# Beta loaded behind the second x segment, and the order of work planned anew

## The chip, the cores and the metric

The kernel runs on one core of a Trainium2 chip. The metric is the device time of one execution in microseconds (us), median over several runs. The engines of the core run their own instruction queues and meet through semaphores: PE does matrix products, DVE and ACT elementwise work (ACT also exponentials and the GELU), POOL elementwise work on SBUF, and SP does nothing but issue DMAs here. PE writes to PSUM, which DVE and ACT read; POOL and the DMAs do not touch it in this kernel.

## The reference

Two branches over the same x (2048 tokens, 512 features) are mixed per token by a gate. Branch A is attention in four segments of 512 tokens with 32 heads of 16, plus a linear memory (M, z) of the earlier segments; `beta` (32 numbers) mixes memory and attention per head. Branch B is a gated feed-forward layer with 1792 hidden features.

```python
g = sigmoid((x * gate_w).sum(-1, keepdims=True))
# branch A, per segment s of 4
qs, ks, vs = q[:, :, s], k[:, :, s], v[:, :, s]
p = softmax(qs @ ks^T * 0.25 + causal_mask)
a_dot = p @ vs
pq = phi(qs)                                  # phi(t) = t + 1 if t > 0 else exp(t)
a_mem = (pq @ M) / (pq @ z + 1e-06)
o = sigmoid(beta) * a_mem + (1 - sigmoid(beta)) * a_dot
M = M + phi(ks)^T @ vs ; z = z + phi(ks).sum(tokens)
a = o @ wo
# branch B
b = (gelu(x @ w_gate) * (x @ w_up)) @ w_down
out = g * a + (1 - g) * b
```

All inputs and the output are bf16.

## The kernel before

The whole sequence stays on the chip: weights, one to three segments of x transposed (`xT`, three buffers), and all intermediate tiles. Work is cut into named tasks of one to 128 instructions. The names are segment and index:

- `K`, `Q`: one of four feature blocks of a projection, 4 matmuls of 128x512 each; `V0_1b`: one of eight value groups (4 matmuls of 256 or 257 columns; the 257th is the token gate, from gate_w). K of segment 0 is cut into parts a, b, c that follow the arrival of x. `Kev`, `Qev`, `Vev` are the evictions from PSUM, on DVE (`:d`) or ACT (`:a`).
- `kpada`, `kpadb` (DVE): K with half of its partitions masked, needed by the scores. `phka`, `phkb`, `phkc`: the three steps of phi(K) (DVE L460, ACT L462, DVE L464); `ktr` its DMA transpose, L572. `phq...` the same for Q.
- `st0_1B` (PE, L601): one fill of score columns into the four banks of `psX`; `exp0_1B` (ACT, L608) its exponential into a `pt` tile, `msk0_1B` (POOL, L614) the causal mask on it. There is one `psX`: the next fill waits for the exponential. A segment has 18 fills. `pv0_1` (PE, L643): the probability-value product of two feature blocks, 128 small matmuls; it needs the masks and `vsh`, a copy of V shifted by 64 partitions, made by DMA (L517). Then `tp`, `pvp`, `ota` (DVE: L529, L666 and L667, L672), where L667 multiplies by `gq` = 1 - sigmoid(beta).
- `mz`, `mza`, `mzq`: memory write; `nd` (PE, L546), `ndp` (DVE, L557 to L560), `otr` (DMA, L563), `otm` (DVE, L674): memory read. L557 uses `gfull`, that is from beta too.
- `G`, `U`: one of 14 hidden blocks of w_gate (`wg`) and w_up (`wu`), 4 matmuls each; `Gev`, `gelu`, `gd`, `h`: eviction, GELU, product. `out0_1_0`: a third of a row block of the product with w_down. `wev`: its eviction times 1 - g; `wo`: product with wo; `oev` (L752) joins both; `dma` stores. Row block 15, the last, is cut into two halves (`wo3_3a`, `wo3_3b`).

All PE products except the scores go through four PSUM banks (`psD`); the digit behind a task in the order is the bank that it opens. A bank can be opened again when its last reader is through.

Nothing is ordered at run time: the string `ORDER`, at the end of the file, lists all tasks, and every engine issues its own tasks in that order. The Emitter adds the semaphore waits that the data require. So a task waits for what it needs and all tasks behind it on the same engine wait with it. The string is the result of an offline planner.

The loads: `ld_x0_1` and `ld_wk0` are issued by ACT, all others by SP. A load can be told to wait for another to have landed (the list at the end of `ld_w`), if that other one stands earlier in the order. Of x, the first two row blocks of segment 0 are transposed on PE (`xtr0`, evicted by `xev0`), all else by DMA transposes (`ld_x0_t2`, `ld_x0_t3`, `ld_x1_0` to `ld_x3_3`). Halves of the weights are `wk0`, `wk1`, `wq0` and so on. `ld_x2_...` waits for `wu1`, `ld_wg0` and `ld_wu0` for `wq1`, `ld_wv` for `x0_t3`, `ld_wu1` for `wg0`.

The gating instructions of beta: `betab` (DVE, L763, four copies), `bexp` (ACT, two exponentials, L775 and L776), `gqa` (POOL), `gqb` (DVE), `gfull` (POOL). Those of the token gate: `gwz`, `ld_gw`, `gwtr`, `gwev` put gate_w into column 512 of wv; `gz`, `gr`, `goa`, `gob`, `goc` make g and 1 - g per segment.

The order of the loads on SP's queue before is: x0_0, wk1, x0_t2, x0_t3, wq0, wq1, gw, beta, wv, wg0, x1_2, x1_1, x1_3, x1_0, wu1, x2_0, vsh0_21, x2_1, x2_3, ktr0_3, wg1, vsh0_01, vsh0_20, x2_2, ktr0_2, vsh0_00, wd1, wd0, wu0, ktr0_1, ktr0_0, and later ones.

Of the kernel before, what the change touches and what calls it, by code (L numbers as in the profile page):

```python
# [876 lines left out]
G1_2:1 U0_0:0 gd0_7 Gev1_2:d pvp0_11 h0_0 U0_13:3 U0_10:2 h0_10 Q2_1:1 Qev2_1:d exp0_2C st0_2D mz0:0 U0_7:2 U0_9:1
pvp0_10 h0_13 exp0_2D phqb1_0 st0_2E exp0_2E phka1_0 h0_7 mza0 h0_9 ota0_0 phqa1_2 kpadb1_0 G1_4:3 U0_1:2 h0_1
Gev1_4:a V1_1b:0 st0_3A G1_0:1 U0_5:3 Q2_2:2 exp0_3A Vev1_1b:a Gev1_0:a Qev2_2:a kpadb1_1 st0_3B exp0_3B U0_11:0
U0_4:1 U0_12:2 st0_3C phkb1_0 exp0_3C phqc1_0 kpada1_2 h0_4 h0_5 U0_6:1 U0_2:3 h0_11 h0_12 phqb1_2 h0_2 G1_3:0  # L880
Gev1_3:d h0_6 kpadb1_2 st0_3D phka1_2 U0_3:2 h0_3 U0_8:3 h0_8 Q2_3:0 Qev2_3:d exp0_3D phkb1_2 msk0_2A msk0_2B msk0_2C
msk0_3A msk0_2E msk0_2D msk0_3C goc0 msk0_3B st1_0A msk0_3D pv0_3:1230 exp1_0A st1_0B exp1_0B tp0_d20 tp0_d21 pvp0_20
tp0_d30 ota0_1 pvp0_21 tp0_d31 kpada1_3 out0_1_0:1 out0_1_1 out0_1_2 V2_0a:2 Vev2_0a:d G1_9:3 V2_1b:0 Vev2_1b:d
wev0_1:d st1_0C G1_8:2 G1_10:0 G1_11:1 gelu1 gd1_9 G1_7:3 gd1_8 gd1_10 gd1_7 gd1_11 G1_13:2 gd1_13 G1_12:0 gd1_12
phqc1_2 phkc1_0 mzq0 pvp0_31 pvp0_30 ota0_3 V2_0b:3 Vev2_0b:d ota0_2 V2_1a:1 Vev2_1a:d out0_0_0:2 out0_0_1 out0_0_2
nd1_0:0 ndp1_0 phkc1_2 exp1_0C st1_0D exp1_0D K2_0:3 K2_2:1 wev0_0:d Kev2_0:d Kev2_2:a K2_1:0 st1_0E Kev2_1:d U1_2:2
h1_2 wo0_1:1 nd1_3:3 nd1_1:0 exp1_0E st1_1A ld_x3_2 vsh1_00 vsh2_01 ktr1_1 ktr1_0 oev0_1 ndp1_1 wo0_0:2 oev0_0
kpada2_0 vsh1_21 out0_2_0:1 nd1_2:0 msk1_0C msk1_0A exp1_1A st1_1B exp1_1B msk1_0B gz1 msk1_0E msk1_1A msk1_0D msk1_1B
out0_2_1 wo0_2:2 ndp1_2 st1_1C exp1_1C nd1_5:0 out0_2_2 ndp1_3 wev0_2:a ndp1_5 out0_3_0:3 st1_1D nd1_4:0 out0_3_1
out0_3_2 ktr1_2 dma0 vsh1_01 otr1_3 ndp1_4 otr1_0 oev0_2 phka2_0 msk1_1C wev0_3:d ktr1_3 dma1 vsh2_00 otr1_1 ld_x3_1  # L890
ld_x3_0 ld_x3_3 exp1_1D st1_2A exp1_2A gr1 msk1_1D pv1_1:1023 st1_2B exp1_2B tp1_d01 tp1_d00 kpadb1_3 V2_2b:0
Vev2_2b:d K2_3:1 Kev2_3:a G2_3:0 pvp1_00 Gev2_3:d tp1_d10 st1_2C U1_8:1 G2_1:0 otr1_2 V2_3a:2 h1_8 Gev2_1:d Vev2_3a:d
kpadb2_0 kpadb2_1 exp1_2C st1_2D phkb2_0 exp1_2D G2_6:1 wo0_3:0 U1_3:2 pvp1_01 tp1_d11 Gev2_6:a h1_3 phka2_2 oev0_3
st1_2E U1_0:3 V2_3b:1 G2_0:2 Gev2_0:d h1_0 Vev2_3b:d exp1_2E phkb2_2 st1_3A mz1:0 G2_4:2 G2_5:3 pvp1_10 mza1 Gev2_5:d
exp1_3A st1_3B exp1_3B Gev2_4:d U1_11:1 G2_2:0 Gev2_2:d ota1_0 U1_13:3 h1_13 U1_10:2 h1_10 h1_11 G2_11:0 G2_10:3
pvp1_11 phkc2_0 phkc2_2 ota1_1 otm1_0 otm1_1 G2_12:2 G2_9:1 st1_3C gelu2 gd2_11 gd2_12 G2_7:0 G2_13:2 gd2_10 gd2_9
gd2_7 gd2_13 G2_8:3 gd2_8 U1_7:1 U2_9:0 K3_0:2 h1_7 U2_5:3 Q3_0:1 phqa2_0 h2_9 h2_5 Qev3_0:d Kev3_0:d exp1_3C st1_3D
exp1_3D U1_1:0 U2_12:3 msk1_3A msk1_2A msk1_3B U2_13:1 h2_12 h1_1 h2_13 kpada2_1 st2_0A U1_9:2 V2_2a:3 U2_7:0 msk1_2D
msk1_2B msk1_2E h1_9 Vev2_2a:d vsh2_20 dma2 dma3 ktr2_0 ktr2_2 vsh2_21 exp2_0A phqb2_0 msk1_3D msk1_2C msk1_3C st2_0B
h2_7 kpada2_2 pv1_3:1230 tp1_d21 exp2_0B tp1_d20 V3_1a:2 Vev3_1a:a st2_0C exp2_0C pvp1_21 tp1_d31 U1_6:1 Q3_1:2  # L900
V3_0a:0 st2_0D h1_6 pvp1_20 Vev3_0a:d Qev3_1:a V3_2b:1 U1_4:2 U1_5:0 exp2_0D st2_0E exp2_0E tp1_d30 phqc2_0 h1_5 h1_4
ota1_2 Vev3_2b:a U1_12:3 h1_12 pvp1_31 pvp1_30 out1_1_0:0 st2_1A V3_1b:2 out1_1_1 V3_3a:3 exp2_1A st2_1B msk2_0B
msk2_0D Vev3_3a:a exp2_1B out1_1_2 U2_4:1 msk2_0E goa1 gob1 kpadb2_3 kpada2_3 msk2_0C msk2_0A msk2_1A ota1_3 h2_4
otm1_2 otm1_3 K3_1:3 mzq1 Vev3_1b:a wev1_1:a st2_1C msk2_1B goc1 U2_1:2 Q3_3:1 V3_0b:0 Kev3_1:d kpada3_0 h2_1 Qev3_3:d
kpadb2_2 exp2_1C msk2_1C st2_1D V3_2a:3 U2_6:2 exp2_1D Vev3_2a:a wo1_1:1 Vev3_0b:d kpadb3_0 h2_6 oev1_1 st2_2A msk2_1D
pv2_1:0231 exp2_2A st2_2B exp2_2B tp2_d00 pvp2_00 phqa2_2 tp2_d01 tp2_d10 pvp2_10 pvp2_01 tp2_d11 out1_0_0:0 out1_0_1
st2_2C phqb2_2 out1_0_2 V3_3b:2 Vev3_3b:d wev1_0:d out1_3_0:3 phqc2_2 pvp2_11 exp2_2C st2_2D exp2_2D wo1_0:1 out1_3_1
st2_2E nd2_0:2 out1_2_0:0 out1_3_2 msk2_2C gz2 gr2 gz3 gr3 goa3 ndp2_0 gob3 oev1_0 msk2_2D goc3 goa2 gob2 exp2_2E
st2_3A exp2_3A msk2_3A msk2_2B wev1_3:d G3_4:2 nd2_2:1 out1_2_1 Gev3_4:a ndp2_2 st2_3B exp2_3B nd2_4:3 G3_1:1 Gev3_1:d
out1_2_2 nd2_1:2 st2_3C dma4 ktr2_1 vsh3_20 vsh3_01 ktr2_3 dma5 ndp2_4 ndp2_1 G3_3:1 wo1_3:3 exp2_3C Gev3_3:a K3_2:2  # L910
st2_3D wev1_2:a msk2_2A kpada3_1 oev1_3 Kev3_2:d nd2_5:1 nd2_3:3 G3_0:0 G3_5:2 ndp2_3 ndp2_5 Gev3_0:d msk2_3C msk2_2E
exp2_3D st3_0A exp3_0A goc2 msk2_3D msk2_3B G3_2:3 wo1_2:1 Gev3_2:d G3_6:0 Gev3_6:a Gev3_5:d oev1_2 ota2_0 st3_0B
pv2_3:3210 exp3_0B tp2_d20 tp2_d21 K3_3:3 Kev3_3:a pvp2_20 pvp2_21 U2_3:2 tp2_d30 h2_3 st3_0C U2_8:3 U2_0:1 tp2_d31
otr2_2 otr2_0 dma6 dma7 otr2_1 vsh3_00 otr2_3 vsh3_21 h2_0 ota2_1 G3_7:2 G3_12:0 G3_10:1 gelu3 gd3_7 h2_8 ota2_2
kpadb3_2 kpadb3_3 pvp2_30 pvp2_31 ota2_3 G3_8:3 gd3_10 gd3_12 gd3_8 G3_9:2 G3_11:1 gd3_11 gd3_9 G3_13:0 U2_11:3 Q3_2:1
U2_10:2 Qev3_2:d h2_10 gd3_13 U2_2:0 U3_13:1 exp3_0C st3_0D exp3_0D h2_2 h2_11 otm2_3 otm2_2 kpadb3_1 otm2_0 otm2_1
# [42 lines left out]
```

## Time and profile before

| | us |
|---|---|
| median of 3 runs | 263.74 (263.47 to 264.35) |
| the profiled execution | 264.53 |
| its span, first to last instruction | 262.8 |
| granted clock of PE in it | 1.000 |
| L601, 512 matmuls of the fills | 28.5 busy |
| L448, 448 matmuls of G and U | 108.0 busy |
| L734, 224 matmuls of out | 53.2 busy |
| L608, 72 exponentials on ACT | 135.1 busy, 1.877 each |
| L614, 128 masks on POOL | 92.6 busy, 0.734 each |
| L529, 32 transposes on DVE | 21.7 busy, 0.701 each |
| vsh copies, issue to landing | 2.0 / 2.9 / 5.8 (least, median, most) |
| transposed loads of x, issue to landing | 2.5 / 3.3 / 8.4 |
| store of 128 KB / 64 KB, issue to landing | 1.8 / 1.6 |

Times in a profile count from the start of the span. Busy times of matmuls overlap where they are pipelined, so the rows of a table like this one do not add up to PE's busy time, and the end of a matmul is modelled. DMA issues appear on the issuing engine's queue (SPq); their landing is a time of its own. The chain of waits goes back from the last instruction to what released it, step by step.

### The profile page before, as it was taken

The page shows a single profiled execution, that of the slowest core. Times are in us where ns is not written, and L with a number is a line of the kernel's source. Part 1 is how long each engine was busy: PE and PEld are TensorE (multiplying, and loading weights), DVE is VectorE, ACT ScalarE, POOL GpSimd, SP SyncE. Part 2 cuts the span into 40 slices and gives each one's busy share as a digit, 9 for nine tenths or more (in the row PEclk, how much of TensorE's full clock was granted, in tenths as well). Part 3 has the DMA queues.
Part 4 walks back from the last instruction along what each step waited for, and adds up shares of the span by engine and source line. Part 5 has one row for each costly group of instructions (what it writes and reads, how often), then busy time and mean ns, then how long its engine had stood idle before and what let it go on. Part 6 is the DMA issues. An engine that isn't in the chain of part 4 may idle for free.

```text
span 262.8 us, 6704 instructions
## 1 busy us (share of the span) xinstructions
PE 257.9 (98%) x2849; PEld 122.5 (47%) x2849; DVE 197.4 (75%) x412; ACT 203.2 (77%) x171; POOL 99.1 (38%) x163
## 2 busy tenths in 40 slices
...
GB/s 186 244 160 144 163 278 275 93 2 1 5 28 2 61 43 39 91 75 2 2 0 71 35 0 2 2 41 61 68 79 0 2 1 22 3 0 42 62 42 80
DMA packets 31974, 16.50 MB, mean 63 GB/s; under 512 B 21576, under 2 KB 31944, under 8 KB 31944
## 3 DMA queue, kind: packets, MB, share of 16 engines
...
## 4 chain that ended last, share of the span: by engine, by line
PE 92%; DMA 4%; SPq 1%; issue 0%; DVE 0%; DVEq 0%
PE psD L448 47%; PE psD L734 19%; PE psX L601 9%; PE psD L643 6%; PE psD L748 5%; PE psD L498 5%; DMA wg<-in_B_w_gate_dram 3%; PE psD L546 1%; DMA wq<-in_A_wq_dram 1%; SPq L361 1%; PE psD L576 1%; SPq L341 1%; DVE ost L752 0%; DVEq L817 0%
## 5 line engine op out<-in xcount | busy, mean ns | idle before, releaser
L608 ACT ACTIVATE pt<-psX 128x2048 bf16<-128x2048 f32 x72 | 135.1, 1877 | 29.5 <-PE psX L601 27.9
L614 POOL TENSOR_TENSOR pt<-pt,ctri 128x256 bf16<-128x256 bf16 x128 | 92.6, 734 | 128.3 <-ACT pt L608 123.8
L448 PE MATMUL psD<-xT,wu 128*128 128x512 bf16 x224 | 54.6, 380 | 0.0
L448 PE MATMUL psD<-xT,wg 128*128 128x512 bf16 x224 | 53.4, 380 | 1.1 <-DMA wg<-in_B_w_gate_dram 1.1
L734 PE MATMUL psD<-wd,gb 128*128 128x512 bf16 x224 | 53.2, 380 | 0.0
L719 DVE TENSOR_TENSOR gb<-psD,gb 128x512 bf16<-128x512 f32 x56 | 37.2, 681 | 10.8 <-PE psD L448 10.7
L448 PEld LDWEIGHTS psD<-xT,wg 128*128 128x128 bf16 x224 | 20.8, 98 | 25.8 <-issue 2.6
L734 PEld LDWEIGHTS psD<-wd,gb 128*128 128x128 bf16 x224 | 20.7, 98 | 24.3 <-issue 2.1
L448 PEld LDWEIGHTS psD<-xT,wu 128*128 128x128 bf16 x224 | 20.2, 98 | 24.7 <-issue 2.6
L601 PE MATMUL psX<-qT,kD 32*128 32x192 bf16 (+7 forms) x512 | 28.5, 287 | 0.0
L529 DVE STREAM_TRANSPOSE tT<-psD 128x512 f32<-128x512 f32 x32 | 21.7, 701 | 5.6 <-PE psD L643 5.1
L442 DVE CAST gb<-psD 128x512 bf16<-128x512 f32 x20 | 13.6, 689 | 13.7 <-PE psD L448 13.7
L601 PEld LDWEIGHTS psX<-qT,kD 32*128 32x128 bf16 x512 | 8.2, 92 | 25.1 <-ACT pt L608 13.4
L498 PE MATMUL psD<-wv,xT 128*128 128x257 bf16 (+1 forms) x128 | 18.2, 273 | 0.0
L752 DVE SCALAR_TENSOR_TENSOR ost<-psD,gtok,wds 128x512 bf16<-128x512 f32 (+1 forms) x17 | 11.9, 711 | 7.7 <-PE psD L748 7.6
L667 DVE SCALAR_TENSOR_TENSOR ob<-tT,gq,rc 128x256 bf16<-128x256 f32 x32 | 16.7, 522 | 1.1
L702 ACT ACTIVATE gb<-psD 128x512 bf16<-128x512 f32 x28 | 15.0, 594 | 3.3 <-PE psD L448 3.3
L643 PE MATMUL psD<-pt,vnat 64*17 64x192 bf16 (+7 forms) x512 | 17.1, 283 | 0.0
L643 PE MATMUL psD<-pt,vsh 64*17 64x192 bf16 (+7 forms) x512 | 17.1, 283 | 0.0
L448 PE MATMUL psD<-xT,wq 128*128 128x512 bf16 x64 | 16.3, 379 | 0.0
L748 PE MATMUL psD<-wo,oT 128*128 128x512 bf16 (+1 forms) x68 | 16.2, 367 | 0.0
L498 PEld LDWEIGHTS psD<-wv,xT 128*128 128x128 bf16 x128 | 11.8, 97 | 6.6 <-issue 1.4
...
## 6 DMA issues: line engine op xcount, KB each, us to landing
...
```

Of the source, the lines that this page charges most:

```text
L448: one(name, PE, n * T_MM, [I(lambda e, i=i: e.matmul(BK[sl.i][:, :], lhs(i), rhs(i), start=(i == 0), stop=(i == n - 1)), reads(i), [bk(sl) ...
L498: one(f"V{s}_{m}{'ab'[hf]}", PE, 2 * T_MM, [I(lambda e, i=i, sl=sl, a=a, z=z, xs=xs: e.matmul(BK[sl.i][:, 0:z - a], xs(i), wv[:, i, a:z], ...
L529: one(f"tp{name}", DVE, 0.605, [I(lambda e, sl=sl, ti=ti: e.transpose(tT[ti][:, :], BK[sl.i][:, :]), [bk(sl)], [("tT", ti)])], bias=bias)
L601: ins.append(I(lambda e, t=t, kb=kb, ncol=ncol, c0=c0, g=g: e.matmul(XALL[:, g * 512 + c0:g * 512 + c0 + ncol], kD[(4 * s + t) % R_KD][32 ...
L608: one(f"exp{s}_{name}", ACT, 2048 * 0.000833 + 0.05, [I(lambda e: e.activation(pt[slot][:, :, :], xin, ACTF.Exp, scale=ATT_SCALE), [("X",) ...
L614: ins.append(I(lambda e, mv=mv: e.tensor_tensor(mv, mv, cm, ALU.mult), [("pt", slot), ("causal",)], [("pt", slot)]))
L643: ins.append(I(lambda e, kb=kb, slot=slot, c0=c0, n=n, g=g, r0=r0, sl=banks[j], va=va: e.matmul(BK[sl.i][32 * g:32 * g + 17, 64 * kb:512], ...
L667: I(lambda e, ti=ti, ri=ri, t=t, j=j, dst=dst: e.scalar_tensor_tensor(out=dst, in0=t_rows(ti), scalar=gq[:, 2 * t + j:2 * t + j + 1], in1= ...
L702: t = one(f"gd{s}_{ft}", ACT, 0.485, [I(lambda e, gi=gi, f=f, sl=sl: e.activation(gb[gi][:, f, :], BK[sl.i][:, :], ACTF.Gelu_apprx_tanh), ...
L719: one(f"h{s}_{ft}", DVE, 0.605, [I(lambda e, sl=sl, gi=gi, f=f: e.tensor_tensor(gb[gi][:, f, :], BK[sl.i][:, :], gb[gi][:, f, :], ALU.mult ...
L734: mm.append(I(lambda e, fb=fb, gi=gi, f=f, q=q, sl=sl: e.matmul(BK[sl.i][:, :], gb[gi][:, f, q], wd[:, fb, :], start=(fb == 0), stop=(fb = ...
L748: one(f"wo{s}_{qt}{sfx}", PE, 4 * T_MM * w / 512, [I(lambda e, kb=kb, q=q, so=so, c=c, w=w: e.matmul(BK[so.i][:, 0:w], oT[:, kb, q], wo[:, ...
```

## The change

One line changes in the code: `ld_beta` waits for `wq1` and not for `wk0`. All else is the string `ORDER`. It lists the same tasks, with the same instructions, in another order, in places with another bank, and some evictions change between DVE and ACT (ACT has 153 tasks and not 156, DVE 333 and not 330).

On SP the order is now: x0_0, wk1, x0_t2, x0_t3, wq0, wq1, gw, wv, wg0, x1_0, x1_2, x1_3, x1_1, beta, ktr0_0, wu1, ktr0_3, vsh0_01, x2_2, wg1, x2_1, vsh0_20, x2_0, vsh0_21, vsh0_00, ktr0_2, x2_3, wu0, ktr0_1, wd0, vsh1_01, wd1, wo, and later ones.

On PE the order up to the fifth fill is now: the K0 parts, Q0_0, Q0_1, st0_0A, gwtr, Q0_3, V0_2a, V0_0b, V0_1b, st0_0B, Q0_2, V0_1a, V0_0a, G0_2, st0_0C, G0_6, V0_3a, G0_1, st0_0D, Q1_1, G0_5, G1_6, st0_0E. Before it was: the K0 parts, Q0_0, Q0_1, st0_0A, gwtr, Q0_3, V0_1b, V0_3a, V0_3b, st0_0B, V0_0b, V0_1a, V0_2a, G0_6, st0_0C, Q0_2, G0_2, V0_2b, st0_0D, V1_2b, V0_0a, G1_6, V1_0b, st0_0E.

`betab` stands on DVE between Vev1_1a and Qev1_0 (before: between Vev0_2a and Gev0_2), `bexp` on ACT behind exp0_1B (before: behind exp0_0D). On POOL gz0 and gqa stand behind the masks msk0_0B, 0C, 0E and 0D (before: ahead of all masks). The first memory write mz0 moves from behind st0_2D to ahead of st1_0A. At the end, wo3_3a and wo3_3b come before wo3_2, with their evictions and stores.

```diff
@@ -364,7 +364,7 @@
     ld_w("wq0", SP, wq[:, halves[0], :], wsrc(A_wq)[:, halves[0], :], [("wq", 0)], 0.25)
     ld_w("wq1", SP, wq[:, halves[1], :], wsrc(A_wq)[:, halves[1], :], [("wq", 1)], 0.25)
     ld_w("wv", SP, wv[:, :, 0:512], wsrc(A_wv), [("wv",)], 0.5, ["x0_t3"])
-    ld_w("beta", SP, ball, A_beta.partition_broadcast(P), [("ball",)], 0.02, ["wk0"])
+    ld_w("beta", SP, ball, A_beta.partition_broadcast(P), [("ball",)], 0.02, ["wq1"])
     ld_xt(1, "wq0")
     ld_w("wg0", SP, wg[:, :, fhalf[0]], wgr[:, :, fhalf[0]], [("wg", 0)], 0.9, ["wq1"])
     ld_w("wg1", SP, wg[:, :, fhalf[1]], wgr[:, :, fhalf[1]], [("wg", 1)], 0.9, ["wu0"])
@@ -859,74 +859,74 @@
 ORDER = """
-ld_x0_0 ld_wk1 ld_x0_1 warm1:0 ident xtr0_1 xev0_1:d xtr0_0 warm2 xev0_0:d vones0 masks ld_wk0 causal1 gwz ld_x0_t2
-ld_x0_t3 ld_wq0 ld_wq1 ld_gw ld_beta causal0 consts K0_1a:1 K0_3a:2 K0_3b K0_2a:3 K0_0a:0 K0_2b K0_0b K0_1b K0_0c
-K0_2c K0_3c K0_1c Kev0_0:d Kev0_2:d kpadb0_0 kpadb0_2 causal kpada0_0 Kev0_3:a Q0_0:0 Qev0_0:a Q0_1:3 st0_0A gwtr:2
-Kev0_1:d gwev Q0_3:0 ld_wv ld_wg0 Qev0_1:d V0_1b:1 V0_3a:2 V0_3b:3 exp0_0A Qev0_3:d Vev0_3a:a Vev0_1b:a st0_0B
-Vev0_3b:d kpada0_2 kpada0_1 V0_0b:0 V0_1a:2 V0_2a:1 Vev0_0b:d G0_6:3 Gev0_6:d Vev0_1a:d Vev0_2a:d exp0_0B st0_0C
-exp0_0C Q0_2:0 G0_2:3 V0_2b:2 ld_x1_2 ld_x1_1 betab ld_x1_3 ld_x1_0 st0_0D Vev0_2b:a exp0_0D Gev0_2:d kpadb0_1
-Qev0_2:d phka0_0 V1_2b:1 V0_0a:3 G1_6:2 V1_0b:0 Vev1_2b:d phka0_2 st0_0E Vev0_0a:d Vev1_0b:d G0_1:1 bexp Gev1_6:a
-exp0_0E Gev0_1:d Q1_2:3 V1_3b:2 V1_3a:0 kpada0_3 Qev1_2:d Vev1_3a:d phkb0_2 phkc0_2 Vev1_3b:d st0_1A gz0 gqa exp0_1A
-gr0 Q1_0:1 V1_0a:3 G1_5:0 Vev1_0a:d gqb Gev1_5:d st0_1B Q1_1:2 K1_0:3 exp0_1B phkb0_0 ld_wu1 ld_x2_0 G0_5:0 Qev1_0:d
-kpadb0_3 vsh0_21 st0_1C exp0_1C Qev1_1:d ld_x2_1 ld_x2_3 ktr0_3 ld_wg1 Gev0_5:d V1_2a:1 K1_3:2 K1_1:0 vsh0_01
-Vev1_2a:a vsh0_20 ld_x2_2 ktr0_2 vsh0_00 ld_wd1 st0_1D phkc0_0 Kev1_1:d kpada1_1 G0_4:1 G0_3:0 Gev0_4:d Kev1_0:d
-Gev0_3:d Kev1_3:a ld_wd0 ld_wu0 ktr0_1 ktr0_0 vsh1_20 ld_wo V1_1a:2 Vev1_1a:d exp0_1D st0_2A exp0_2A msk0_0B msk0_0D
-msk0_0C kpada1_0 msk0_0E goa0 gob0 msk0_0A msk0_1A msk0_1C msk0_1D gfull msk0_1B G0_0:1 Q1_3:3 G1_1:0 Qev1_3:d phqa1_0
...
-oev2_0 pvp3_10 nd3_5:1 msk3_2B msk3_2A msk3_2D msk3_2E msk3_3A ndp3_3 wev2_2:d h3_5 exp3_3B st3_3C exp3_3C wo2_2:2
-out3_1_0:3 st3_3D out3_1_1 nd3_4:0 out3_1_2 dma8 exp3_3D msk3_3B msk3_2C msk3_3C msk3_3D wev3_1:a ota3_0 ndp3_5 oev2_2
-ndp3_4 ota3_1 dma11 otr3_2 otr3_1 otr3_3 otr3_0 pv3_3:1203 tp3_d20 tp3_d21 pvp3_20 pvp3_21 tp3_d30 tp3_d31 ota3_2
-pvp3_31 pvp3_30 otm3_1 otm3_0 ota3_3 out3_0_0:1 out3_2_0:2 out3_0_1 out3_2_1 out3_3_0:0 out3_0_2 out3_3_1 wev3_0:a
-otm3_2 otm3_3 wo3_0:3 dma10 oev3_0 dma12 wo3_1:1 out3_2_2 out3_3_2 wo3_2:3 oev3_1 wev3_2:a oev3_2 wo3_3b:1 dma13 dma14
-wev3_3:a oev3_3b dma15b wo3_3a:2 oev3_3a dma15a
+gwz ld_x0_1 causal0 ld_x0_0 ld_wk1 ld_x0_t2 causal1 ident warm1:0 xtr0_1 consts ld_x0_t3 ld_wk0 xev0_1:d xtr0_0 warm2
+K0_0a:1 xev0_0:a K0_2a:2 K0_3a:3 K0_3b K0_2b masks K0_1a:0 K0_0b K0_1b K0_0c K0_3c K0_1c K0_2c Kev0_0:d kpadb0_0
+Kev0_2:d kpada0_0 Kev0_1:a kpada0_2 ld_wq0 ld_wq1 ld_gw Q0_0:1 ld_wv Q0_1:0 Qev0_0:a st0_0A exp0_0A kpadb0_1 Kev0_3:d
+gwtr:2 Q0_3:1 ld_wg0 ld_x1_0 ld_x1_2 ld_x1_3 ld_x1_1 ld_beta vones0 gwev Qev0_1:d V0_2a:3 V0_0b:2 V0_1b:0 Vev0_0b:a
+Qev0_3:d phka0_2 phka0_0 Vev0_2a:a Vev0_1b:d kpada0_1 kpada0_3 st0_0B Q0_2:1 V0_1a:2 V0_0a:3 G0_2:0 exp0_0B Vev0_1a:d
+Vev0_0a:d Gev0_2:d phkb0_0 st0_0C exp0_0C G0_6:2 V0_3a:3 G0_1:0 st0_0D Gev0_6:d kpadb0_2 causal Vev0_3a:d Qev0_2:a
+phkc0_0 exp0_0D phkb0_2 Q1_1:2 G0_5:1 Gev0_1:d Qev1_1:d Gev0_5:d G1_6:3 Gev1_6:d kpadb0_3 phkc0_2 st0_0E V0_3b:0
+K1_1:2 G1_1:1 Kev1_1:d Vev0_3b:d Gev1_1:d exp0_0E st0_1A G1_5:3 V1_1a:2 Q1_2:0 exp0_1A st0_1B exp0_1B Qev1_2:d
+Vev1_1a:d betab bexp Q1_0:1 V0_2b:0 G0_3:2 Qev1_0:d msk0_0B msk0_0C Gev1_5:a st0_1C msk0_0E msk0_0D Vev0_2b:d V1_1b:1
+Vev1_1b:d Gev0_3:d K1_2:0 V1_0a:3 V1_0b:1 exp0_1C st0_1D Vev1_0a:a gz0 gr0 V1_3b:2 Vev1_3b:d phqa1_0 Vev1_0b:a G0_4:3
+Q1_3:1 Kev1_2:d ktr0_0 exp0_1D st0_2A exp0_2A Qev1_3:d ld_wu1 ktr0_3 vsh0_01 ld_x2_2 ld_wg1 gqa msk0_1C msk0_0A
+msk0_1A gfull msk0_1D goa0 msk0_1B G0_0:2 V1_3a:0 K1_3:1 Vev1_3a:a gqb Gev0_0:d Gev0_4:d Kev1_3:d ld_x2_1 st0_2B
+vsh0_20 ld_x2_0 vsh0_21 vsh0_00 ktr0_2 ld_x2_3 ld_wu0 ktr0_1 ld_wd0 vsh1_01 ld_wd1 ld_wo pv0_1:2031 exp0_2B tp0_d01
+tp0_d00 K1_0:0 Q2_0:2 st0_2C pvp0_01 Kev1_0:d tp0_d11 Qev2_0:d pvp0_00 tp0_d10 G0_13:0 G0_12:1 G0_7:2 G0_8:3 gelu0
...
+st3_3A pvp3_01 tp3_d11 ndp3_4 nd3_5:2 out2_2_1 wo2_3:0 pvp3_10 oev2_0 ndp3_5 exp3_3A st3_3B exp3_3B msk3_2C msk3_2D
+msk3_3A msk3_2E out2_2_2 U3_11:3 wo2_2:2 st3_3C pvp3_11 wev2_2:d h3_11 oev2_3 U3_5:1 otr3_0 dma8 otr3_1 otr3_3
+out3_1_0:3 exp3_3C st3_3D exp3_3D msk3_2B msk3_3B goc3 msk3_3C msk3_2A otr3_2 oev2_2 h3_5 out3_1_1 out3_1_2 ota3_0
+ota3_1 otm3_0 wev3_1:a msk3_3D pv3_3:0213 otm3_1 tp3_d20 tp3_d21 pvp3_21 pvp3_20 tp3_d31 tp3_d30 pvp3_30 pvp3_31
+out3_3_0:0 out3_3_1 out3_2_0:2 out3_0_0:3 out3_0_1 out3_0_2 out3_2_1 wev3_0:a dma11 dma10 ota3_2 otm3_2 ota3_3 otm3_3
+wo3_1:1 oev3_1 dma13 wo3_0:3 oev3_0 out3_3_2 wo3_3a:1 wo3_3b:3 out3_2_2 dma12 wev3_3:d oev3_3b oev3_3a dma15b dma15a
+wev3_2:a wo3_2:0 oev3_2 dma14
```

96 lines of the change are left out of this document (47 added, 49 removed).

## The prediction

> **What bounds the kernel now.** I read four views in this order: busy time per engine, the windows, the chain of waits, and then the timeline of the first 17 and the last 7 us. Busy time comes first:
>
> ```profile
> span 262.8 us, 6704 instructions
> PE 257.9 (98%) x2849; PEld 122.5 (47%) x2849; DVE 197.4 (75%) x412; ACT 203.2 (77%) x171; POOL 99.1 (38%) x163
> ```
>
> A share of 98% asks for one thing only: where are the missing 4.9 us? The windows answer it (us, then busy us of PE, PEld, DVE, ACT, POOL with instruction counts, granted clock, DMA share, GB/s):
>
> ```profile
> 11.63:15.03 3.40, 3.39 (x34) 2.37 (x32) 2.34 (x8) 3.33 (x5) 0.00 (x0) 1.00 1.66 238
> 15.03:16.12 1.09, 0.00 (x1) 0.03 (x2) 0.00 (x0) 0.51 (x1) 0.00 (x0) 1.00 0.50 92
> 16.12:259.06 242.94, 242.94 (x2703) 111.01 (x2704) 189.25 (x390) 196.24 (x163) 95.54 (x142) 1.00 0.24 54
> 259.06:262.80 3.74, 0.77 (x8) 0.45 (x5) 1.47 (x3) 0.00 (x0) 0.00 (x0) 1.00 0.23 70
> ```
>
> From 16.12 to 259.06 PE is busy for all of 242.94 us at clock 1.00: a new order can gain nothing there and can only lose. What is left is one hole of 1.09 us at 15.03, the start-up ahead of it and the tail. The chain says what the hole waits for (start, us, what):
>
> ```profile
> 4.98 3.47 DMA wq<-in_A_wq_dram
> 8.47 7.51 DMA wg<-in_B_w_gate_dram
> 16.12 1.02 PE psD L448 x4
> ```
>
> The first half of the gate weights (wg0) is issued at 8.47, when wq1 has landed, and lands at 15.98. The first gate group starts 0.14 later.
>
> **Beta's move.** Beta goes from eighth to fourteenth on SP's queue: past wv, wg0 and the four transposes of x1. Around it SP's timeline reads:
>
> ```profile
> 6.31 0.37 SPq L341 DMA_DIRECT2D omem<-in_A_beta_dram  x1
> 6.73 0.42 SPq L341 DMA_DIRECT2D wv<-in_A_wv_dram  x1
> 8.47 0.37 SPq L341 DMA_DIRECT2D wg<-in_B_w_gate_dram  x1
> 8.88 7.11 SPq L345 DMA_TRANSPOSE xT<-in_A_x_dram  x4
> 16.04 0.58 SPq L341 DMA_DIRECT2D wu<-in_B_w_up_dram  x1
> 22.01 1.13 SPq L345 DMA_TRANSPOSE xT<-in_A_x_dram  x1
> ```
>
> The issue slot is worth 6.73 - 6.31 = 0.42 us to wv. The DMA columns (the last two) say more:
>
> ```profile
> 6.50:7.50 1.00, 1.00 (x12) 0.90 (x10) 0.00 (x0) 0.00 (x0) 0.00 (x0) 1.00 0.96 333
> 7.50:8.30 0.80, 0.80 (x9) 0.72 (x8) 0.67 (x2) 0.00 (x0) 0.00 (x0) 1.00 0.29 88
> 8.30:9.00 0.70, 0.70 (x8) 0.53 (x6) 0.70 (x3) 0.49 (x1) 0.00 (x0) 1.00 0.28 81
> 9.00:10.00 1.00, 1.00 (x6) 0.45 (x5) 1.00 (x5) 0.30 (x2) 0.00 (x0) 1.00 0.94 329
> ```
>
> The stream runs at 330 GB/s, falls to 85 for 1.5 us just when beta's 128 rows of 64 bytes pass (issued 6.31, landing 3.8 later), and recovers. That dip holds 1.5 x (1 - 85/330) = 1.1 us of lost stream. Beta may cause all of it, or only the part that its issue slot explains, the rest being wv's own delay from issue to first byte. So wv, and behind it wg0, come 0.4 to 1.1 us earlier; 0 is the floor if wg0's issue, which waits for wq1 at 8.45, decides alone. I take 0.8, nearer the upper end, because beta ahead is the only odd thing in the dip. wg0 then lands at 15.2.
>
> The Trainium skill speaks against this: "DMA: Bandwidth & Descriptors", section "Anatomy of one DMA — SWDGE (gpsimd) path", calls descriptor generation small and says that many descriptors can be emitted before the cost shows up. By it 128 rows more cost nothing and wg0 still lands at 15.98; this is rival A below. The dip beside beta's rows bears it out only in part, and these loads are not on the path that the section describes.
>
> Beta's consumers now come later. The copies into betab (4 instructions, 0.73 together, at 18.45 on DVE) stand behind the eviction of V1_1a, about 28 us; beta, issued at about 15, needs the 3.8 it took before. The exponentials (0.20 and 0.22 on ACT, at 21.90) follow the fill 0_1B. What needs them is the first L667, at 42.3. On POOL gz0 and gqa now stand behind four masks, where before gz0 held that queue for 15.4 us; POOL is 38% busy. All this costs nothing under PE's work. Without that cover the price would be the 0.7 us of betab.
>
> **The order before the first gate group.** Ahead of it PE had Q0_0, Q0_1, Q0_3 and six V groups; now it has Q0_2 as well and five V groups. A Q group takes 0.86 and a V group 0.44 (chain of waits), so 0.42 us of work that came later now lies in front of the hole. PE arrives at 15.03 + 0.42 = 15.45. With wg0 at 15.2, and 0.14 to start, it doesn't wait: 1.09 us gained. Bounds: no earlier landing leaves 16.12 - 15.45 = 0.67 of wait and a gain of 0.42; more than 1.09 there is not to be had. Before that point nothing moves: both kernels start K0 when wk lands, its 32 matmuls take 3.4 us, and the second eviction of x0 (now ACT; its 128x512 evictions take 0.60 against 0.43 on DVE) is wanted only after six more matmuls of 0.107, 0.64. If that cover failed it would cost 0.2.
>
> **The middle.** Every group keeps its size. After a fill, a probability-value pass or a memory write the next dense group takes 0.97 instead of 0.86; the old order returns so 70 times, the new one 69: -0.11. ACT keeps up by a sum per fill: back to back, an exponential takes 1.76, an L442-like eviction on ACT 0.55, a phi exponential 1.05 against 2.6 to 3.0 of PE work, and no fill of the new order asks for more than its PE work by over 0.05. No gain, no loss, with the conditions named under the rivals.
>
> **The tail.** Before, PE and DVE end so:
>
> ```profile
> 257.93 1.90 PE L748 MATMUL psD<-wo,oT 128*128 128x512 bf16 x12
> 259.00 1.54 DVE L752 SCALAR_TENSOR_TENSOR ost<-psD,gtok,wds 128x512 bf16<-128x512 f32 x3 [1.84 <-PE psD L748]
> ```
>
> Last come the two half tiles of row block 15. Now they go first and the whole wo3_2 is last. PE ends with the same work; L752 on a whole tile (0.71) starts at once, as its ACT factor (0.69) runs beside wo3_2 (0.86). DVE so ends 0.76 behind PE, where it was 260.54 - 259.83 = 0.71. The last store is 128 KB (1.8 to land) and no longer 64 KB (1.6): +0.2 with the difference above, bounds -0.1 and +0.5. Ahead of it the new order does two of the four additions L674 before the last probability-value pass, so the DVE chain that ended at 254.40, with wo3_0 at 254.48, has 0.7 us of air.
>
> **The sum.** -1.09 - 0.11 + 0.20 = -1.0. The profiled execution took 264.53 (span 262.8 and 1.73 around it), so 263.53 by its own time; the runs' median, 263.74, is 0.79 lower, which gives **262.7**. With the bounds of its terms (0.42 to 1.09, -0.1 to 0.5): 262.4 to 263.8.
>
> **Rival A: wg0 lands no earlier.** For it: wg0 is issued only after wq1, and its last third shares the engines with the transposes of x1 (13 to 15: 172 GB/s at a DMA share of 2.12). Against it: the dip. The gain is 0.42 + 0.11 - 0.20 = 0.3: 263.4, no change.
>
> **Rival B: SP's queue comes late (slower).** The new queue puts a transpose of phi(K), ktr0_0, ahead of wu1. It needs the last phi step on DVE, which now stands behind the eviction of V0_3a: PE ends V0_3a at about 18.0, DVE has Gev0_6, a pad, the causal copy, the eviction and 1.22 of L464 left: 20.6; the transpose takes 1.26. So wu1 is issued at 22.0 and not at 16.04, and behind it on SP wait x2_2 (for wu1 to have landed), wg1, x2_1 and the vsh copies of segment 0, the last of which is issued 5.7 us after wu1 has landed (three transposes of 1.28, two vsh of 0.63, wg1 0.59 and gaps) and lands 2.9 later. PE wants it for pv0_1 at 39.5 - 0.42 - 1.09 = 38.0. The point that decides: wu1 landing later than 29.4. Loads of wu took 5.96 and 10.66 us: 28.0 is in time, 32.7 costs 3.3 and gives 262.7 + 3.3 = 266.0. For it: the margin is 1.4 us. Against it: the slower load had two 0.9 MB loads ahead, and wu1 will have only one transpose; Q2_0, which needs the last x2, has 2 us of air.
> The Trainium skill, same page, section "Rules for kernel authors", says to issue a DMA early and wait late; by it this move is a risk without a return. The trace agrees so far as wu1, issued at 16.04, made x2 wait 5.4 us on SP and PE never.
>
> **Rival C: short waits of PE in the new order.** The four PSUM banks must be free in time everywhere. One place: behind the fill 0_1B DVE has Qev1_2 0.68, Vev1_1a 0.42, betab 0.73 and Qev1_0 0.68, 2.5 us, against Q1_0, V0_2b, G0_3 and a fill, 2.6 of PE. Before, not one such wait showed in 243 us. Some four to six waits of 0.2 to 0.4 would add 0.8 to 2.2: about 264.2.
>
> **How the numbers follow.** Forecast 0.46, A 0.17, B 0.14, C 0.23. About 0.3%, 0.8 us, is what a measurement of this kernel can tell from no change: faster means below 262.95. Faster: the forecast without its upper edge, 0.42. Same: A, a third of C and that edge, 0.30. Slower: B and the rest of C, 0.28. The range goes from 262.0, with the tail at its better bound and the run's own spread, up to 265.2, over C and into B.
>
> **What would show it.** First gate matmul at or before 15.6 with no wait for wg; no dip to 85 GB/s ahead of wv; PE fully busy in one window from the first gate group to the tail; wu1 issued at about 22, vsh of segment 0 landed before pv0_1. Wrong would be: a wait of PE for wg of over 0.3 us (A), any idle time of PE before L643 at 38 us (B), or a window in the middle where PE is below its length (C).

## The result, and the profile after

| | before | after |
|---|---|---|
| median of 18 runs each | 264.25 (263.47 to 264.75) | 265.12 (264.62 to 267.09) |
| the profiled execution | 264.53 | 265.30 |
| its span | 262.8 | 263.6 |

All times here are in us. The ratio after to before is 1.0038, with a 95% interval of 1.0025 to 1.005: the change makes the kernel 0.87 slower, where 262.7 had been forecast, 1.0 faster than the median then known. 265.12 lies inside the range of the prediction, at its upper edge, which had been stretched there for its rivals C and B.

The head of the page after, as before: span, then busy time, share and instructions of each engine.

```profile
span 263.6 us, 6712 instructions
PE 258.5 (98%) x2849; PEld 123.0 (47%) x2849; DVE 202.3 (77%) x415; ACT 201.4 (76%) x168; POOL 99.1 (38%) x163
```

PE is still the bound, at the same share; 0.8 of span is too little to see in a share. PE around the place where the hole was (start, duration, what):

```profile
14.82 1.04 PE L498 MATMUL psD<-wv,xT 128*128 128x256 bf16 x8
15.70 1.02 PE L448 MATMUL psD<-xT,wg 128*128 128x512 bf16 x4
16.66 0.40 PE L601 MATMUL psX<-qT,kD 32*128 32x384 bf16 x8
```

The first gate group starts at 15.70, right behind the value groups, with no wait. The hole of 1.09 is gone. SP's timeline, with beta now behind wv, wg0 and the four transposes of x1:

```profile
6.46 0.39 SPq L341 DMA_DIRECT2D wv<-in_A_wv_dram  x1
8.52 0.37 SPq L341 DMA_DIRECT2D wg<-in_B_w_gate_dram  x1
8.94 5.29 SPq L345 DMA_TRANSPOSE xT<-in_A_x_dram  x4
14.28 0.58 SPq L341 DMA_DIRECT2D omem<-in_A_beta_dram  x1
```

wv is issued 0.27 earlier, wg0 lands at 14.35 and not at 15.98. Yet the span is longer, so the time must be lost behind it. The windows from the first gate group to the end (us, then busy us of PE, PEld, DVE, ACT, POOL with instruction counts, granted clock, DMA share, GB/s):

```profile
15.70:181.50 165.80, 165.80 (x1820) 76.78 (x1817) 131.01 (x265) 140.68 (x121) 65.80 (x97) 1.00 0.26 59
181.50:187.50 6.00, 5.18 (x35) 2.13 (x34) 5.37 (x15) 4.12 (x3) 5.74 (x9) 1.00 0.26 53
187.50:226.00 38.50, 38.50 (x479) 17.19 (x481) 30.00 (x60) 32.68 (x27) 12.63 (x20) 1.00 0.23 37
226.00:228.00 2.00, 1.74 (x97) 1.01 (x76) 1.67 (x4) 1.50 (x2) 0.30 (x1) 1.00 0.06 16
228.00:260.44 32.44, 32.44 (x309) 14.61 (x307) 26.45 (x54) 15.14 (x10) 11.08 (x17) 1.00 0.19 40
260.44:263.60 3.16, 0.02 (x1) 0.00 (x0) 0.75 (x1) 0.00 (x0) 0.00 (x0) 1.00 0.19 62
```

Two windows in the middle are not full: 0.82 is missing in the second, 0.26 in the fourth. Before, there was no such window. This is the prediction's own sign of rival C. PE's waits name the partners (engine, line, what it waited for: us in total, times, longest):

```profile
PE psX L601 <- DVE kD L487: 0.7, 1, 0.7
PE psX L601 <- ACT pt L608: 0.3, 1, 0.3
PE psD L546 <- DVE omem L560: 0.2, 1, 0.2
```

In order of time these are: the memory read nd2_4 at 181.55, which waits 0.16 for a PSUM bank that ndp2_2 (L560) still reads; the fill st3_0A at 186.75, which waits 0.66 for the mask of K (kpada3_0, L487); the fill st3_2C at 227.23, which waits 0.26 for exp3_2B, late on ACT behind an eviction (wev2_3). Together 1.08. The longest, on PE and then on DVE:

```profile
184.86 1.89 PE L448 MATMUL psD<-xT,wg 128*128 128x512 bf16 x8
187.41 0.40 PE L601 MATMUL psX<-qT,kD 32*128 32x512 bf16 x4 [0.66 <-DVE kD L487]
```

```profile
183.76 0.75 DVE L742 TENSOR_SCALAR wds<-psD,omgt 128x512 f32<-128x512 f32 x1 [0.46 <-PE psD L734]
184.43 0.83 DVE L487 TENSOR_SCALAR kD<-kT,maskA 128x512 bf16<-128x512 bf16 x1
...
186.01 0.67 DVE L487 TENSOR_SCALAR kD<-kT,maskB 128x512 bf16<-128x512 bf16 x1
186.60 0.75 DVE L487 TENSOR_SCALAR kD<-kT,maskA 128x512 bf16<-128x512 bf16 x1
```

DVE works without a pause up to the end of kpada3_0, and PE starts 0.06 behind it. The three L487 take 0.83, 0.67 and 0.75, where the median of this line is 0.35. All that time POOL runs score masks, eleven in a row from 180.78 to 188.6:

```profile
180.78 7.84 POOL L614 TENSOR_TENSOR pt<-pt,ctri 128x256 bf16<-128x256 bf16 x11 [5.21 <-ACT pt L608]
```

At the start, one difference is not in the program. The K0 products, before and then after:

```profile
5.25 3.65 PE L476 MATMUL psD<-xT,wk 128*128 128x256 bf16 x32
```

```profile
5.11 4.22 PE L476 MATMUL psD<-xT,wk 128*128 128x256 bf16 x32
```

In the profile after, the first five start 0.21 apart and nearly all others 0.109, so Q0_0 starts at 9.16 and not at 8.74. Two more profiles of the kernel before (below) show three and five such matmuls: it changes from execution to execution. The Trainium skill, "TensorE: Matmul & The Clock Gate", Part 1, says that the number of cold matmuls (those at half clock) at the start varies from run to run and is not to be fitted. The profiles here agree that the number varies, from 0 to 7; that the clock is the reason is not shown, as the granted clock reads 1.00 there.

The tail came near the forecast: PE ends at 260.46 and the span 3.12 later, where it was 2.98: +0.14 for +0.20. DVE ends 0.79 behind PE (before 0.70), and the last store takes 1.69 to land (before 1.63); the prediction had taken the medians of the two sizes, 1.8 and 1.6.

### The profile page after: what moved, and what is told of

Read it like the earlier page. It is cut to its first block, busy times and chain, and to the rows that moved or that the text cites. A ratio compares the mean times of both kernels' runs of the same rounds, so it can differ in the third digit from the quotient of the medians.

```text
span 263.6 us, 6712 instructions
## 1 busy us (share of the span) xinstructions
PE 258.5 (98%) x2849; PEld 123.0 (47%) x2849; DVE 202.3 (77%) x415; ACT 201.4 (76%) x168; POOL 99.1 (38%) x163
## 4 chain that ended last, share of the span: by engine, by line
PE 91%; POOL 3%; DVE 2%; ACT 1%; issue 0%; DVEq 0%
PE psD L448 46%; PE psD L734 16%; PE psX L601 8%; PE psD L498 6%; PE psD L643 6%; PE psD L748 5%; POOL pt L614 3%; PE psD L476 2%; ACT pt L608 1%; PE psD L382 1%; PE psD L546 1%; DVE kD L487 1%; PE psD L576 1%; DVE omem L560 1%; DVE rcm L559 0%
## 5 line engine op out<-in xcount | busy, mean ns | idle before, releaser
L734 PE MATMUL psD<-wd,gb 128*128 128x512 bf16 x224 | 54.0, 380 | 0.0
L719 DVE TENSOR_TENSOR gb<-psD,gb 128x512 bf16<-128x512 f32 x56 | 37.5, 683 | 10.8 <-PE psD L448 10.4
L702 ACT ACTIVATE gb<-psD 128x512 bf16<-128x512 f32 x28 | 15.5, 595 | 3.8 <-PE psD L448 3.6
L442 DVE CAST gb<-psD 128x512 bf16<-128x512 f32 x21 | 14.0, 679 | 4.3 <-PE psD L448 4.3
L667 DVE SCALAR_TENSOR_TENSOR ob<-tT,gq,rc 128x256 bf16<-128x256 f32 x32 | 16.4, 514 | 1.1
```

The costliest lines, as they stand in the source:

```text
L667: I(lambda e, ti=ti, ri=ri, t=t, j=j, dst=dst: e.scalar_tensor_tensor(out=dst, in0=t_rows(ti), scalar=gq[:, 2 * t + j:2 * t + j + 1], in1= ...
L702: t = one(f"gd{s}_{ft}", ACT, 0.485, [I(lambda e, gi=gi, f=f, sl=sl: e.activation(gb[gi][:, f, :], BK[sl.i][:, :], ACTF.Gelu_apprx_tanh), ...
L719: one(f"h{s}_{ft}", DVE, 0.605, [I(lambda e, sl=sl, gi=gi, f=f: e.tensor_tensor(gb[gi][:, f, :], BK[sl.i][:, :], gb[gi][:, f, :], ALU.mult ...
L734: mm.append(I(lambda e, fb=fb, gi=gi, f=f, q=q, sl=sl: e.matmul(BK[sl.i][:, :], gb[gi][:, f, q], wd[:, fb, :], start=(fb == 0), stop=(fb = ...
```

## The experiments

Twelve runs were made, in four groups, each group on a chip of its own; "against" gives the time of the kernel before in the same group. In the diffs of the order a line is cut to the tasks that move. Theories are numbered in the expectations; each text says what its theories hold.

**Beta alone.** Is the load's move worth what was forecast, without the new order? e1 is the kernel before with only the load moved.

```diff
-    ld_w("beta", SP, ball, A_beta.partition_broadcast(P), [("ball",)], 0.02, ["wk0"])
+    ld_w("beta", SP, ball, A_beta.partition_broadcast(P), [("ball",)], 0.02, ["wq1"])
-ld_wq0 ld_wq1 ld_gw ld_beta causal0
+ld_wq0 ld_wq1 ld_gw causal0
-ld_x1_2 ld_x1_1 betab ld_x1_3 ld_x1_0 st0_0D
+ld_x1_2 ld_x1_1 ld_x1_3 ld_x1_0 ld_beta betab st0_0D
```

> The old order with one thing of the change: beta is loaded behind the four transposes of x1 (waiting for wq1). Its gating instructions keep their old places, so betab stands third behind the first gate eviction on DVE. Theory 1 (beta's move alone frees the load stream, and all that the changed kernel loses lies in the new order behind it): wg0 lands near 14.5 and not at 15.98, PE's hole of 1.09 us at 15.0 closes, and the kernel gains: 263.2 to 263.6 against 264.25. betab, reached by DVE at about 17.4, waits for beta, which landed at 18.0 in the changed kernel: up to 0.7 us on DVE, part of which PE may feel. Rival (wg0's early landing comes from the rest of the new order): the hole stays, 264.2.

Measured: 264.53 against 264.23, ratio 1.001 (0.9996 to 1.0024). The hole is gone (wg0 lands at 15.07), but nothing is won, as PE now waits elsewhere:

```profile
PE psD L476 <- DMA wk<-in_A_wk_dram: 0.4, 1, 0.4
PE psD L498 <- DVE gb L442: 0.3, 1, 0.3
```

Beta lands at 18.82, betab waits for it on DVE, and an eviction (L442) queued behind betab holds a bank that PE wants at 20.08:

```profile
18.85 0.73 DVE L763 COPY betab<-omem 32x8 bf16<-32x8 bf16 x4 [0.85 <-DMA omem<-in_A_beta_dram]
19.61 0.69 DVE L442 CAST gb<-psD 128x512 bf16<-128x512 f32 x1
```

The first of PE's two rows is the arrival of wk, which no edit here touches; it also makes PE late for wg0. In e2 beta's consumers are moved back as well, still in the old order (the changed wait, and beta's absence from its old place, are as in e1):

```diff
-betab ld_x1_3 ld_x1_0 st0_0D
+ld_x1_3 ld_x1_0 ld_beta st0_0D
-G0_1:1 bexp Gev1_6:a
+G0_1:1 Gev1_6:a
-st0_1A gz0 gqa exp0_1A
+st0_1A gz0 exp0_1A
-Vev1_0a:d gqb Gev1_5:d
+Vev1_0a:d Gev1_5:d
-st0_1D phkc0_0 Kev1_1:d
+st0_1D phkc0_0 betab Kev1_1:d
-exp0_1D st0_2A
+exp0_1D bexp st0_2A
-msk0_1D gfull
+msk0_1D gqa gfull
-exp0_2B tp0_d01
+exp0_2B gqb tp0_d01
```

> As the run before it, but the gating instructions are placed with slack: betab on DVE behind phkc0_0 (about 32 us), the exponentials on ACT behind exp0_1D, gqa on POOL just ahead of gfull, gqb on DVE ahead of the first transposition of segment 0. Theory 1: PE's hole closes and nothing waits, 263.1 against 264.25, a gain of 1.1. If slack matters, this run is faster than the one before it by up to 0.7; if it doesn't, both are equal within 0.2.

Measured: 263.90 against 264.23, ratio 0.9983 (0.9965 to 1.0001), and PE full from the first gate group to the tail:

```profile
16.00:259.00 243.00, 243.00 (x2706) 111.19 (x2704) 190.64 (x391) 196.31 (x163) 94.74 (x142) 1.00 0.25 53
```

So the move with slack seems to pay, but about 0.3 and not 1.09, and the interval still touches 1. The last group repeats it on another chip:

> The kernel e2_beta_slack once more, on another chip. Theory 1 (beta's load ahead of wv holds back wg0, and the kernel before waits 0.2 to 1.1 us for it, 0.59 on the mean of its three profiles; the load moved, with its consumers late enough, takes that wait away and adds none): 0.2 to 0.5 us under the kernel before, 263.5 to 263.9, no idle time of PE over 0.1 us between 16 us and the tail. Theory 2 (what e2_beta_slack showed was chance, wg0's landing varies by as much with beta behind as ahead): within 0.15 of the kernel before, and a hole ahead of the first gate group again.

Measured: 263.90 against 264.40, ratio 0.9974 (0.9963 to 0.9984). The interval lies below 1, so the gain is there, and PE is full behind 16 us; but the wait at the hole is not gone in every execution, as this profile shows:

```profile
PE psD L448 <- DMA wg<-in_B_w_gate_dram: 0.4, 1, 0.4
```

**Beta back in the new order.** e3 is the changed kernel with beta's load where it was.

```diff
-    ld_w("beta", SP, ball, A_beta.partition_broadcast(P), [("ball",)], 0.02, ["wq1"])
+    ld_w("beta", SP, ball, A_beta.partition_broadcast(P), [("ball",)], 0.02, ["wk0"])
-ld_wq0 ld_wq1 ld_gw Q0_0:1
+ld_wq0 ld_wq1 ld_gw ld_beta Q0_0:1
-ld_x1_3 ld_x1_1 ld_beta vones0
+ld_x1_3 ld_x1_1 vones0
```

> The changed kernel with beta put back ahead of wv (waiting for wk0), all else as changed. Theory 1: wg0 lands at about 15.9 again; PE, which has 0.42 us more work ahead of it now, waits 0.3 to 0.7 us for it: 265.4 to 265.9 against 265.12 of the changed kernel. Rival: landing and time stay as in the changed kernel.

Measured: 265.29 (265.22 to 265.48), ratio 1.0038 (1.0025 to 1.005), as the changed kernel. The rival came true in the time. wg0 lands at 15.22 and PE arrives at 15.59: no wait. In this execution Q0_2 ahead of the gate groups covers wg0 by itself (with 0.37 to spare), and beta's place gives nothing that these runs can tell. The three waits of the middle are all there, so they belong to the order and not to beta.

**The wait of st3_0A.** e4 takes the two masks of K out of the crowded stretch.

```diff
-pv2_1:2103 tp2_d01
+pv2_1:2103 kpadb3_0 kpada3_0 tp2_d01
-ndp2_5 kpadb3_0 wo1_2:3 kpada3_0 Gev3_1:a
+ndp2_5 wo1_2:3 Gev3_1:a
```

> The changed kernel with kpadb3_0 and kpada3_0 moved forward on DVE, from behind ndp2_5 (184 to 187 us, under the bunched masks on POOL) to ahead of tp2_d01 (162 us, where DVE idles 0.8 us and POOL has no mask). Theory 2 (PE's wait of 0.66 us before st3_0A comes from two half-tile maskings of K that take 0.67 and 0.75 there and 0.34 elsewhere, behind a full DVE queue): the wait is gone, L487 takes 0.34 at the new place, and 0.5 to 0.7 us are gained: 264.5 against 265.12. Rival (the wait only moves to the next late task on DVE): the time stays within 0.2 of 265.12.

Measured: 264.70, ratio 1.0017 (1.0006 to 1.0029): 0.42 less than the changed kernel. The wait of 0.66 is gone and the two others stay. At the new place kpada3_0 takes 0.34 but kpadb3_0 0.65; PE waits for neither. Why was DVE late at the old one? e5 leaves POOL's score masks of blocks 3 and 4 of the third segment out (that part of the causal mask is not applied) and touches nothing on DVE:

```diff
-        for (t, kb, ncol, c0) in steps:
+        for (t, kb, ncol, c0) in (() if s == 2 and name[0] in "23" else steps):
```

> The changed kernel without the causal masks (L614, POOL) on the fills of the third and fourth feature block of segment 2, 16 of 128 masks; everything else, the places of kpadb3_0 and kpada3_0 too, as in the changed kernel. Theory 4 (the maskings of K, L487, took 0.67 to 0.83 us at 184 to 187 us because POOL worked on its masks at the same time; elsewhere they take 0.34): L487 takes 0.34 there, and PE's wait of 0.66 us before st3_0A falls to 0.1 or less. Rival (these L487 are slow by themselves or the DVE queue is full anyway): L487 at 0.7 and the wait at 0.5 or more.

Measured: one run, 264.79. DVE in the same stretch, the same rows as above:

```profile
183.96 0.75 DVE L742 TENSOR_SCALAR wds<-psD,omgt 128x512 f32<-128x512 f32 x1 [0.54 <-PE psD L734]
184.62 0.35 DVE L487 TENSOR_SCALAR kD<-kT,maskA 128x512 bf16<-128x512 bf16 x1
...
185.71 0.34 DVE L487 TENSOR_SCALAR kD<-kT,maskB 128x512 bf16<-128x512 bf16 x1
185.97 0.35 DVE L487 TENSOR_SCALAR kD<-kT,maskA 128x512 bf16<-128x512 bf16 x1
```

The same instructions take 0.35, 0.34 and 0.35, L742 (which reads PSUM) takes 0.75 in both, and PE's wait for L487 is gone. So POOL's masks beside them slow these DVE instructions to twice their time, and that is the wait. The other places say the same: over all fourteen profiles the 278 L487 with no mask beside them took 0.31 to 0.35, and the 113 with masks beside them for at least 80% of their time had a median of 0.75. The Trainium skill, "GPSIMD Engine Reference", section "Specifications", says that POOL's interfaces to SBUF are shared with DVE, with contention for DVE instructions with two SBUF inputs or in a two-port mode; the runs agree that the two engines contend, and give it a price for L487, which goes from SBUF to SBUF: 0.34 alone, 0.67 to 0.83 here beside masks. Whether L487 runs in such a mode no profile says.

**The other waits.** e6 is e4 with nd2_4 behind G3_1 and the tail in the old order.

```diff
-nd2_5:2 nd2_4:3 G3_1:1 out1_2_2
+nd2_5:2 G3_1:1 nd2_4:3 out1_2_2
-wo3_0:3 oev3_0 out3_3_2 wo3_3a:1 wo3_3b:3 out3_2_2 dma12 wev3_3:d oev3_3b oev3_3a dma15b dma15a wev3_2:a wo3_2:0 oev3_2 dma14
+wo3_0:3 oev3_0 dma12 out3_2_2 out3_3_2 wev3_2:a wo3_2:1 oev3_2 dma14 wev3_3:a wo3_3b:3 oev3_3b dma15b wo3_3a:2 oev3_3a dma15a
```

> The changed kernel with three mendings: kpadb3_0 and kpada3_0 early as before (264.70), nd2_4 behind G3_1 on PE, so that the four bank reads of ndp2_2 are through when it opens bank 3 (a gap of 0.16 us), and the tail in the old order, wo3_2 ahead of the halves of row block 15 (from PE's last matmul to the end of the span 2.97 us before, 3.16 in the changed kernel). Theory 2 (the loss of the new order is a sum of such single waits): 264.70 - 0.16 - 0.19 = 264.35. Rival (each wait removed turns up further on): 264.7.

Measured: 264.07 against 264.08, ratio 0.9998 (0.9981 to 1.0014). It ran on another chip than e4; by the ratios to before it is 0.5 less than e4 (0.35 was expected) and no different from the kernel before. e10 goes for the last wait:

```diff
-wev2_1:d nd3_0:0 ndp3_0 wo2_1:1 oev2_1 out2_3_2 nd3_3:2
+wev2_1:d out2_3_2 nd3_0:0 ndp3_0 wo2_1:1 oev2_1 nd3_3:2
```

> The changed kernel as in e6_mended, and out2_3_2 ahead of nd3_0, so that wev2_3 runs on ACT right behind exp3_2A and exp3_2B no longer starts late. Theory 4 (the new order is slower only by its short waits, each of which is worth its own length): the idle time of 0.26 us at 226 us is gone and no other comes, 263.8 (e6_mended minus 0.26), 0.3 under the kernel before. The rival (a wait mended moves on: the outputs, the memory read and the probability-value pass share four banks, and DVE is the next to be late): 264.05 +- 0.1 as e6_mended, with an idle time of 0.1 to 0.4 of PE within 5 us behind.

Measured: 264.88 against 264.40, ratio 1.0017 (1.0005 to 1.0029), 0.5 worse than e6 by the ratios, though the two intervals touch. The wait was not cured, as the rival had said:

```profile
PE psX L601 <- ACT pt L608: 0.3, 1, 0.3
PE psD L643 <- DVE rcm L557: 0.3, 1, 0.3
```

The eviction oev2_1 now ends 0.6 later on DVE (at 224.02). wev2_3 on ACT (at 224.11) and pv3_1 on PE (at 224.17) start right behind it, so the old wait stays and a new one of 0.27 stands ahead of it; that oev2_1 holds them is read from the times and the banks, as the row names L557, which runs next on DVE. This profile is of the fastest of e10's twelve runs (264.30), so what makes the median slower is only in part seen in it.

**How lucky was the first profile?** The hole of 1.09 came from one execution. The kernel before was profiled twice more, unchanged (b1, b2).

> The kernel before, unchanged, for a second profile. Theory 3 (the first profile of it began well: its K0 ran at full speed from the first matmul, 0.108 us each, where the five other profiles of this study have 3 to 6 matmuls at 0.21, and Q0_0 began at 8.74 against 9.04 to 9.46; so its hole of 1.09 us was larger than in most executions, since wg0 lands at its own time): here Q0_0 begins at 9.0 to 9.5 and the hole is 0.3 to 0.8 us, with wg0 landing at 15.5 to 16. Rival (the first profile is typical): Q0_0 at 8.7, hole 1.1.

> The kernel before, unchanged, for a third profile; the same expectations as for the second one: by theory 3 Q0_0 begins at 9.0 to 9.5 and the hole ahead of the first gate group is 0.3 to 0.8 us, by its rival 8.7 and 1.1.

Measured: 264.10 and 264.95. Both holes were smaller than 1.09, as theory 3 has it, but b1's 0.17 is a wait for wv, and wg0 landed at 14.63 and 16.31, outside the 15.5 to 16 that it expected. What their traces and the others show at the start:

| profile | Q0_0 begins | first matmuls at about 0.21 | wg0 lands | PE idle ahead of the first V or gate groups | Q0_0 + idle |
|---|---|---|---|---|---|
| before | 8.74 | 0 | 15.98 | 1.09 | 9.83 |
| before, b1 | 9.03 | 3 | 14.63 | 0.17 | 9.20 |
| before, b2 | 9.65 | 5 | 16.31 | 0.51 | 10.16 |
| e1 | 9.46 | 3 | 15.07 | 0 | 9.46 |
| e2 | 9.15 | 5 | 15.17 | 0 | 9.15 |
| e9 | 8.87 | 0 | 15.43 | 0.41 | 9.28 |
| after | 9.16 | 5 | 14.35 | 0 | 9.16 |
| e3 | 9.05 | 4 | 15.22 | 0 | 9.05 |
| e4 | 9.32 | 3 | 14.61 | 0 | 9.32 |
| e5 | 9.35 | 7 | 14.56 | 0 | 9.35 |
| e6 | 8.42 | 0 | 15.35 | 0.28 | 8.70 |
| e10 | 8.65 | 0 | 14.98 | 0 | 8.65 |

wg0's landing varies by 1.7 in one and the same kernel, and so does the moment when PE gets there; a late start of PE hides a late weight. The hole of 1.09 was an early start that met a late landing. The last column is what counts: 9.73 on the mean for before. The next two kernels were to set PE's start itself, with ten more warm-up products, in the kernel before (e7) and in e2 (e8).

```diff
-    for name, n, cols in (("warm1", 45, 80), ("warm2", 7, 80)):
+    for name, n, cols in (("warm1", 45, 80), ("warm2", 17, 80)):
```

> The kernel before with ten more of the warming matmuls (80 columns) between the transposes of x0 and K0, so that PE starts K0 some 0.5 us later. Theory 3: the hole ahead of the first gate group takes up what PE is late, the time stays within 0.2 us of 264.23. Rival (the start is on the path that sets the end): 264.7.

> The old order with beta behind x1 and its gating instructions placed with slack (263.9), and the same ten warming matmuls more. Theory 3: without the hole nothing takes up the late start, and the time rises by 0.4 to 0.7: 264.3 to 264.6. Rival: it stays at 263.9.

Measured: 265.77 against 264.08 (ratio 1.0064, 1.0044 to 1.0084) and 265.24 (1.0048, 1.003 to 1.0066). Both missed what was expected, for the edit did not do what it was for. In their profiles Q0_0 does not start later but at 8.40 and 8.69, with no matmul at 0.21, and PE's longest wait is a new one, e7's here:

```profile
PE psD L448 <- issue: 1.6, 1, 1.6
PE psD L498 <- DMA wv<-in_A_wv_dram: 0.9, 1, 0.9
```

At 44.61 PE stands still for 1.57 (e8: 0.75 at 43.81) and waits for no semaphore that the profile shows. So these two say nothing about the start. The traces do point at a cause. In both the stop stands ahead of the same instruction, the 962nd of PE's records, and a 16 KB transfer that the trace marks as instructions (queue 8, 22 of them in an execution) had ended 1.50 (e7) and 1.29 (e8) before PE went on. In the twelve other profiles PE reaches its 962nd record 1.31 to 5.5 after that transfer and does not stop. So PE may have waited for its own instructions, which ten more products and their weight loads made it reach too early. No run tested this. e8's profile is of the fastest of its twelve runs (264.20), so the stop need not be all that the median of 265.24 lost.

## Why the prediction was wrong

The table shows where the 2.42 between 262.7 and 265.12 come from, in the prediction's own terms; the column "measured" is worked out from the profiles.

| step | forecast | measured | off by |
|---|---|---|---|
| the profiled execution over the median | 0.79 | 0.28 | 0.51 |
| start and hole | -1.09 | -0.70 | 0.39 |
| PE's own work | -0.11 | +0.14 | 0.25 |
| "The middle", waits | 0 | +1.08 | 1.08 |
| tail | +0.20 | +0.14 | -0.06 |

Their errors add up to 2.17; the other 0.25 is not explained, and is less than what single executions of one kernel differ by.

**The step that failed is the middle: "No gain, no loss".** It was tested with a sum per fill on ACT, and on DVE at one place only, under rival C. The three waits come from the queues of DVE and ACT between fills, and e4 and e6, which take two of them away (and undo the tail), bring the time back to that of the kernel before (264.07 against 264.08), while e3, which undoes the beta part, brings nothing. This is rival C, given 0.23 and a price of 0.8 to 2.2 in "four to six waits"; there were three, worth 1.08, and not at the place it named, but in the last two segments. The third wait was not cured by e10. The longest could have been foreseen in part: with 0.35 for each L487, DVE is done at 186.3 and PE gets there at 186.9 (e5). Only with the times under POOL's masks is it late. The profile before showed that spread, with L487 up to 0.82 against a median of 0.35, but the prediction took one duration for a line.

**The hole was mis-sized.** The load behind beta does land earlier: in all nine profiles with beta behind x1 wv landed at 10.6 to 11.0, in the five with beta ahead at 11.2 to 12.4, a gain of 0.9 between the means, where 0.8 was taken. For wg0 the means differ by 0.5 (15.4 and 14.9), but the ranges overlap (14.6 to 16.3 and 14.3 to 15.4), so rival A, that wg0 lands no earlier, is not refuted by the landings alone; the gain of e9 speaks against it. The issue slot, counted as 0.42, gave next to nothing: without beta ahead, SP waits 0.5 to 0.6 for x0_t3 instead (e1, e2, after), and wv is issued at 6.2 to 6.8 with beta behind and at 6.4 to 6.8 with beta ahead. What became shorter is the time from wv's issue to its landing, 4.4 on the mean with beta behind and 5.1 with beta ahead. And -1.09 was one execution's hole. Over three profiles of before Q0_0 plus idle is 9.73; over after, e3, e4, e5, e6 and e10 it is 9.04: -0.70, of which 0.15 is that Q0_0 began earlier, and that time changes by 0.9 between executions of the kernel before. In the old order (e1, e2, e9) it is 9.30, a gain of 0.43, next to the 0.33 and 0.50 that e2 and e9 measured. And in e3's profile the later arrival of PE, the step "15.03 + 0.42", closes the hole alone; in e6, which starts early, 0.28 of it is there even with beta behind.

**The base.** The sum was moved down by 0.79, from the profiled execution to a median of three runs. With fifteen more the median is 264.25, and the profiled execution only 0.28 above it. So the three known before were low.

**PE's own work.** From Q0_0 to PE's end, less all idle time over 0.08, before's three profiles take 250.0, 250.2 and 250.1 (mean 250.08), the new order's six 250.2 to 250.35 (mean 250.22). The saving of 0.11 for one return fewer does not show.

**Right were** the closing of the hole with no wait (the first gate group at 15.70, where 15.6 was set), the tail within its bounds (+0.14 for +0.20), and SP's queue. wu1 was issued at 22.28 for 22.0 and landed at 28.73, just within the 29.4 that rival B set as its limit; PE was full up to 181.5, so B did not happen:

```profile
22.28 0.58 SPq L341 DMA_DIRECT2D wu<-in_B_w_up_dram  x1
24.81 1.20 SPq L572 DMA_TRANSPOSE phkt<-phk  x1
26.06 0.72 SPq L517 DMA_DIRECT2D vsh<-vnat  x1
28.75 1.14 SPq L345 DMA_TRANSPOSE xT<-in_A_x_dram  x1
```

The dip in the load stream, by contrast, only became shallower (124 and 196 GB/s in the two windows that had 88 and 81), so beta was at most a part of it and not all.
